# The last 1024 tokens of an attention and two-MLP kernel: gate and value as one 2x2 block product with seven multiplications

## The chip, the core and the metric

One core of a Trainium2 chip runs the whole program. The metric is device time in microseconds (us) of one launch, the median of several runs; lower is better. Beside it stands one profiled execution, from which every row below is taken. TensorE (PE, with its weight loads as PEld) multiplies; VectorE (DVE), ScalarE (ACT) and GpSimd (POOL) do the rest; SyncE (SP) issues all DMAs.

## The reference, cut to what matters

```python
# q, k, v: (4, 8, 576, 64) float32; attention over a window of 64 positions
scores = scale * np.matmul(q, k.transpose(0, 1, 3, 2))
scores = np.where((rel >= 0) & (rel < 64), scores, -1e9)
attn = np.exp(scores - max); attn = attn / (attn.sum(-1) + 1e-9)
x = (attn @ v) as (2304 tokens, 512)
# first MLP, d_ff = 1536; the weights are float64
x = (1 / (1 + np.exp(-(x @ w_gate)))) * (x @ w_val) @ w_out
# second MLP
out = ((x @ w_a) * (x @ w_b)) @ w_out2
```

## The kernel before

**Numbers in two parts.** Each MLP operand is held as a high part (`h`) and the remainder (`l`) in fp32r. A product `w x` is three matmuls: high by high, high by low, low by high (`product`, L299 to L309). The float64 weights come in as pairs of 32-bit words and are turned into float32 on the chip (`decode`, L252 to L286: ACT, DVE and POOL), split, used, and also written to DRAM (`kept`). There are 12 chunks of 128 hidden units (`fc`) in each MLP, so 24 decodings of three matrices (gate or `a`, value or `b`, and `o` for out).

**Two halves.** The 2304 tokens are nine blocks of 256. `HALVES` (L32) gives blocks 0 to 4 to the first half, in groups (0), (1, 2), (3, 4), and blocks 5 to 8, the last 1024 tokens, to the second half, in groups (5, 6) and (7, 8). A half runs the first MLP (phase 0) and then the second (phase 1). The first half decodes the weights as it needs them; the second half reads them back from DRAM (`fetch`, L288). A turn of the plan takes one group and three chunks: for each chunk `hidden` (L311) makes gate and value, of 12 matmuls each, one PSUM bank each, with ACT and DVE forming the hidden vector and its two parts; then `projection` (L462) multiplies the hidden parts of the turn before by `o` and adds them to an accumulator in SBUF (`evacuate`, L353). A matmul has 512 columns for a group of two blocks and 256 for a single block. In phase 0 the projection goes block by block with 256 columns, in phase 1 with 512.

**Attention.** 36 units (`attention`, L102: 128 tokens and four heads each) run as generators beside the MLP work. Blocks 0 to 4 come first; those of blocks 5 and 6 are fed in during phase 1 of the first half and those of blocks 7 and 8 at its end and in phase 0 of the second half. A unit ends by writing the two parts of its result, `xh` on ACT and `xl` on DVE (L186, L187).

**Order.** The code is written in one order; the framework's scheduler then lists the instructions of each engine by its own estimate of time, and each engine runs its list strictly in that order. PSUM has eight banks: two for accumulation (`ps_acc`), three for gate and value (`ps_gv`), three for attention (`ps_at`).

Of the kernel before, what the change touches and what calls it, by code (L numbers as in the profile page):

```python
# [8 lines left out]
F32 = mybir.dt.float32  # L9
# [10 lines left out]
def tile_window_attention_gated_mlps(ctx, tc, q, k, v, w1g, w1v, w1o, w2a, w2b, w2o, out):  # L20
    nc = tc.nc
# [10 lines left out]
    HALVES = (((0,), (1, 2), (3, 4)), ((5, 6), (7, 8)))  # L32
    W = 2 * N
    LAG = 1
# [6 lines left out]
    const = ctx.enter_context(tc.tile_pool(name="const", bufs=1))  # L41
    stage = ctx.enter_context(tc.tile_pool(name="stage", bufs=3))
    dec = ctx.enter_context(tc.tile_pool(name="dec", bufs=1))
    wts = ctx.enter_context(tc.tile_pool(name="wts", bufs=G + 1))
    xs = ctx.enter_context(tc.tile_pool(name="xs", bufs=1))
    accp = ctx.enter_context(tc.tile_pool(name="accp", bufs=5))
    hp = ctx.enter_context(tc.tile_pool(name="hp", bufs=5))
    tmp = ctx.enter_context(tc.tile_pool(name="tmp", bufs=2))
    kts = ctx.enter_context(tc.tile_pool(name="kts", bufs=5))
    vs = ctx.enter_context(tc.tile_pool(name="vs", bufs=5))  # L50
    work = ctx.enter_context(tc.tile_pool(name="work", bufs=3))
    small = ctx.enter_context(tc.tile_pool(name="small", bufs=5))
    dram = ctx.enter_context(tc.tile_pool(name="dram", bufs=1, space=bass.MemoryType.DRAM))
    ps_acc = ctx.enter_context(tc.tile_pool(name="ps_acc", bufs=2, space=PSUM))
    ps_gv = ctx.enter_context(tc.tile_pool(name="ps_gv", bufs=3, space=PSUM))
    ps_at = ctx.enter_context(tc.tile_pool(name="ps_at", bufs=3, space=PSUM))
# [9 lines left out]
    mask_n = const.tile([P, P], F32, name="mask_n")  # L66
    mask_0 = const.tile([P, P], F32, name="mask_0")
# [21 lines left out]
    qts = [const.tile([P, 2, 2, 2, WIN], F32, name=f"qt{i}") for i in range(3)]  # L89
# [12 lines left out]
    def attention(t, hq, xhi, xlo, c0):  # L102
# [71 lines left out]
        pt = work.tile([P, 2, 4, WIN], F32, tag="pt", name=f"pt{t}_{hq}")  # L174
# [5 lines left out]
        for i in range(4):  # L180
# [5 lines left out]
        nc.scalar.activation(out=xhi[:, pairs, c0:c0 + P], in_=xps, func=AF.Copy)  # L186
        nc.vector.tensor_tensor(  # L187
            out=xlo[:, pairs, c0:c0 + P], in0=xps, in1=xhi[:, pairs, c0:c0 + P].bitcast(F32), op=ALU.subtract
        )
# [3 lines left out]

    PLACE = {(0,): 0, (1, 2): 1, (3, 4): 2, (5, 6): 3, (7, 8): 1}
# [12 lines left out]
    group_of = {b: g for half in HALVES for g in half for b in g}  # L207

    def attention_units(blk):
        if (0, (blk,)) not in x:  # L210
            new_x(0, group_of[blk])
        for i in range(TB):
            for hq in range(2):
                yield blk, attention(blk * TB + i, hq, *x[0, (blk,)], i * P)
# [21 lines left out]
    staged, ready, kept = {}, {}, {}  # L236

    def load_weights(F):
        ph, fc = divmod(F % (2 * NF), NF)
# [12 lines left out]
    def decode(F):  # L252
# [3 lines left out]
        for nm in "abo":  # L256
# [5 lines left out]
            ex = dec.tile([P, DM], I32, tag="ex", name="ex")  # L262
# [20 lines left out]
            kept[F, nm] = dram.tile([P, 2, DM], F32, tag=f"k{nm}{F}", name=f"k{nm}{F}")  # L283
# [4 lines left out]
    def fetch(F):  # L288

        got = {}  # L290
        for nm in "abo":
            pair = wts.tile([P, 2, DM], F32R, tag=f"w{nm}", name=f"w{nm}")
            nc.sync.dma_start(out=pair.bitcast(F32), in_=kept[F - 2 * NF, nm])
            got[nm] = (pair[:, 0, :], pair[:, 1, :])
        ready[F] = got
        yield


    def product(ps, w, x):  # L299
# [4 lines left out]
        for c in range(NP):  # L304
            for a, b in ((wh, xh), (wh, xl), (wl, xh)):
                nc.tensor.matmul(  # L306
                    ps, lhsT=a[:, c * P:(c + 1) * P], rhs=b[:, c, :], start=(n == 0), stop=(n == 3 * NP - 1)
                )
                n += 1  # L309

    def hidden(phase, w, x):  # L311
# [13 lines left out]
        factor = 0.5 if phase == 0 else 1.0  # L325
        hh = hp.tile([P, W], F32R, tag="hh", name="hh")[:, 0:n]
        hl = hp.tile([P, W], F32R, tag="hl", name="hl")[:, 0:n]
        nc.scalar.activation(out=hh, in_=hr, func=AF.Copy, scale=factor)  # L328
        nc.vector.scalar_tensor_tensor(  # L329
            out=hl, in0=hr, scalar=factor, in1=hh.bitcast(F32), op0=ALU.mult, op1=ALU.subtract  # L330
        )
        return hh, hl
# [54 lines left out]
    def turns(order, half, ph):  # L387
# [3 lines left out]
        def take(group, n):  # L391
            f0 = at[group[0]]
            n = min(n, NF - f0)
# [5 lines left out]
        if (half, ph) == (0, 0):  # L399
            for _, b, fcs in FIRST:  # L400
                take((b,), len(fcs))
        elif ph == 0:
            for g in order:
                for b in g:
                    take((b,), G)
        for j, g in enumerate(order):
            take(g, 1 + j * (G - 1) // (len(order) - 1))
        while any(f < NF for f in at.values()):
# [5 lines left out]
    for half, groups in enumerate(HALVES):  # L414
        order = groups
        for ph in range(2):
            ts = turns(order, half, ph)
            plan.extend((half, ph, g, fcs) for g, fcs in ts)
            order = [g for g, fcs in ts if fcs[-1] == NF - 1]
    base = lambda half, ph: (2 * half + ph) * NF  # L420
# [111 lines left out]
```

## Time and profile before

| | |
|---|---|
| median of 3 runs | 1029.39 us (1029.35 to 1031.32) |
| the profiled execution | 1031.98 us, its span 1030.2 us |
| PE busy | 1008.6 us, 98% of the span, 6278 matmul records |
| DVE, ACT, POOL busy | 543.7, 382.8, 242.0 us |
| chain that ended last | PE 84%, DVE 9%, ACT 3% |
| DMA | 137.64 MB, mean 134 GB/s |

Matmuls overlap in their pipeline, so a busy PE is not PE at its best: the time that one matmul really takes from the stream is the distance between the starts of two neighbours. A record's own length is longer than that.

### The profile page before, as it was taken

How to read it: one execution, taken by the hardware profiler on the slowest of the kernel's cores; microseconds unless marked ns; L12 is line 12 of the kernel's file. 1: busy time of each engine (PE TensorE's matmuls, PEld its weight loads, DVE VectorE, ACT ScalarE, POOL GpSimd, SP SyncE). 2: the span in 40 equal slices, each digit the busy share in tenths (PEclk: the TensorE clock that was granted, in tenths of full speed). 3: DMA queues.
4: the chain of work that ended last, by engine and by line, in shares of the span. 5: the costliest groups of instructions: out<-in, count | busy, mean ns of one | idle time of the engine just before them, and what ended most of it. 6: DMA issues, size and time to landing. Idle time of an engine off the chain costs nothing.

```text
span 1030.2 us, 16412 instructions
## 1 busy us (share of the span) xinstructions
PE 1008.6 (98%) x6278; PEld 887.0 (86%) x6278; DVE 543.7 (53%) x1126; ACT 382.8 (37%) x931; POOL 242.0 (23%) x209
## 2 busy tenths in 40 slices
PE   7899999999999899999999999999999999999998
PEld 6798998989889788888888889988888888888886
DVE  5899468776858975766754354223222221222223
ACT  7887643333334566343321346321111232111110
POOL 2555045433426733333521000000000020000000
PEclk9899999999999999999999999999999999999999
DMA  8998355543534554454524262152232323232102
GB/s 202 246 267 258 68 176 199 177 152 123 205 108 159 164 164 153 142 156 144 205 82 142 86 185 70 42 185 72 74 124 78 123 83 102 82 102 82 62 21 81
DMA packets 114862, 137.64 MB, mean 134 GB/s; under 512 B 62048, under 2 KB 90976, under 8 KB 114784
## 3 DMA queue, kind: packets, MB, share of 16 engines
q1 hardware_dynamic: 114784, 136.60, 42.3%
q8 instruction: 49, 0.80, 0.3%
q14 instruction: 29, 0.24, 0.1%
HBM read 89.65 MB, written 42.47 MB: 128 GB/s over the span
## 4 chain that ended last, share of the span: by engine, by line
PE 84%; DVE 9%; ACT 3%; issue 2%; POOL 2%; DMA 1%; SPq 0%; POOLq 0%; DVEq 0%; ACTq 0%
PE acc L345 26%; PE gps L306 26%; PE vps L306 25%; PE sps L147 2%; PE xps L183 2%; PE tps L173 1%; DVE ex L263 1%; DVE wi L270 1%; DVE ex L275 1%; DVE hl L329 1%; ACT pr L161 1%; PE kqps L120 1%; DVE wi L267 1%; DVE xacc L364 1%; POOL wi L273 1%
## 5 line engine op out<-in xcount | busy, mean ns | idle before, releaser
L306 PE MATMUL gps<-xh,wa 128*128 128x512 f32 (+1 forms) x1056 | 303.8, 355 | 1.0 <-ACT wa L280 1.0
L306 PE MATMUL vps<-xh,wb 128*128 128x512 f32 (+1 forms) x1056 | 301.1, 352 | 0.5 <-ACT wb L280 0.5
L306 PEld LDWEIGHTS gps<-xh,wa 128*128 128x128 f32 x1056 | 190.9, 190 | 27.6 <-ACT wa L280 1.3
L306 PEld LDWEIGHTS vps<-xh,wb 128*128 128x128 f32 x1056 | 190.2, 190 | 27.1 <-ACT wb L280 0.7
L306 PE MATMUL gps<-xl,wa 128*128 128x512 f32 (+1 forms) x528 | 186.7, 354 | 0.8 <-DVE xl L187 0.7
L306 PE MATMUL vps<-xl,wb 128*128 128x512 f32 (+1 forms) x528 | 185.8, 352 | 0.0
L345 PE MATMUL acc<-hh,wo 128*128 128x256 f32 x864 | 166.0, 284 | 1.0 <-DVE xacc L364 1.0
L328 ACT ACTIVATE hh<-hr 128x512 fp32r<-128x512 f32 (+1 forms) x132 | 73.1, 554 | 213.5 <-DVE hr L324 115.2
L345 PEld LDWEIGHTS acc<-hh,wo 128*128 128x128 f32 x864 | 138.2, 191 | 2.8 <-DVE xacc L364 1.1
L345 PE MATMUL acc<-wo,hh 128*128 128x512 f32 x432 | 133.5, 391 | 2.4 <-DVE xacc L364 1.6
L345 PE MATMUL acc<-hl,wo 128*128 128x256 f32 x432 | 122.5, 284 | 1.2 <-DVE hl L329 1.2
L364 DVE TENSOR_TENSOR xacc<-acc,xacc 128x512 f32<-128x512 f32 x130 | 88.1, 688 | 63.2 <-PE acc L345 62.7
L324 DVE TENSOR_TENSOR hr<-vps,hr 128x512 f32<-128x512 f32 (+1 forms) x60 | 38.1, 636 | 150.0 <-PE vps L306 149.3
L273 POOL TENSOR_TENSOR wi<-wi,low 128x512 int32<-128x512 int32 x72 | 98.4, 1366 | 66.1 <-DVE wi L270 42.9
L306 PEld LDWEIGHTS gps<-xl,wa 128*128 128x128 f32 x528 | 100.4, 190 | 13.3 <-DVE xl L187 1.0
L306 PEld LDWEIGHTS vps<-xl,wb 128*128 128x128 f32 x528 | 100.2, 190 | 13.1
L329 DVE SCALAR_TENSOR_TENSOR hl<-hr,hh 128x512 fp32r<-128x512 f32 (+1 forms) x132 | 84.3, 639 | 50.7 <-ACT hh L328 50.3
L321 DVE SCALAR_TENSOR_TENSOR hr<-hr,vps 128x256 f32<-128x256 f32 (+1 forms) x72 | 39.7, 551 | 128.6 <-PE vps L306 125.3
L345 PEld LDWEIGHTS acc<-wo,hh 128*128 128x128 f32 x432 | 80.1, 188 | 19.3 <-DVE xacc L364 1.6
L345 PEld LDWEIGHTS acc<-hl,wo 128*128 128x128 f32 x432 | 82.7, 191 | 2.4 <-DVE hl L329 1.4
L345 PE MATMUL acc<-wo,hl 128*128 128x512 f32 x216 | 83.7, 390 | 0.0
L370 POOL TENSOR_TENSOR xl<-xacc,xh 128x512 fp32r<-128x512 f32 x18 | 25.3, 1419 | 208.7 <-ACT xh L369 208.7
(68 smaller groups left out, 1100.2 us busy)
## 6 DMA issues: line engine op xcount, KB each, us to landing
st_o<-in_moe_w_out_dram SPq DMA_DIRECT2D x24, 512.0 KB, 3.8
ka<-wa SPq DMA_DIRECT2D x24, 512.0 KB, 2.6
kb<-wb SPq DMA_DIRECT2D x24, 512.0 KB, 3.1
ko<-wo SPq DMA_DIRECT2D x24, 512.0 KB, 2.8
wa<-ka SPq DMA_DIRECT2D x24, 512.0 KB, 3.3
wb<-kb SPq DMA_DIRECT2D x24, 512.0 KB, 3.4
wo<-ko SPq DMA_DIRECT2D x24, 512.0 KB, 4.0
st_a<-in_moe_w_gate_dram SPq DMA_DIRECT2D x12, 512.0 KB, 4.3
```

The costliest lines, as they stand in the source:

```text
L120: nc.tensor.transpose(kqps[:, i, j, :], raw[nm][:, 2 * j:2 * j + 2, :], ident)
L147: nc.tensor.matmul(sps[:, s, j, :], lhsT=qt[:, j, s], rhs=kt[:, j, s * WIN:s * WIN + P], start=True, stop=True)
L183: nc.tensor.matmul(xps[rows, i // 2, s * WIN:(s + 1) * WIN], lhsT=vv[:, i, :], rhs=pt[:, s, i, :], start=True, stop=True)
L273: nc.gpsimd.tensor_tensor(out=wi, in0=wi, in1=low, op=ALU.add)
L306: nc.tensor.matmul(ps, lhsT=a[:, c * P:(c + 1) * P], rhs=b[:, c, :], start=(n == 0), stop=(n == 3 * NP - 1))
L321: nc.vector.scalar_tensor_tensor(out=hr, in0=hr, scalar=1.0, in1=vps, op0=ALU.add, op1=ALU.mult)
L324: nc.vector.tensor_tensor(out=hr, in0=vps, in1=hr, op=ALU.mult)
L328: nc.scalar.activation(out=hh, in_=hr, func=AF.Copy, scale=factor)
L329: nc.vector.scalar_tensor_tensor(out=hl, in0=hr, scalar=factor, in1=hh.bitcast(F32), op0=ALU.mult, op1=ALU.subtract)
L345: nc.tensor.matmul(ps, lhsT=a[:, m * P:(m + 1) * P], rhs=b, start=begin and n == 0 and (phase == 1 or m % 2 == 0), stop=end and n == 2 and ...
L364: nc.vector.tensor_tensor(out=dst, in0=ps, in1=dst, op=ALU.add)
L370: nc.gpsimd.tensor_tensor(out=xl, in0=dst, in1=xh.bitcast(F32), op=ALU.subtract)
```

## The change

The code for blocks 5 to 8 is replaced. The first part (`FRONT`, blocks 0 to 4) keeps its plan, except that group (0) stops three chunks short of the end of phase 1.

- **Attention.** All 36 units run in the first part; those of blocks 5 to 8 are paced evenly over the turns from the seventh to the last but two. For these 16 units only one float32 result is written (`xq`, on ACT), without the split.
- **Decoding.** `decode` also stores the float32 of `a` and `b` (`kf`, 48 more DMAs of 256 KB); the buffer `ex` becomes two deep, `pt` goes from three buffers to two.
- **Second pool layout.** `second_part` closes the pools of attention and decoding and opens others in their place.
- **The block product.** The 1024 tokens are two halves of 512 columns; the 512 contraction rows are two halves of 256. Gate and value of a chunk are then a 2x2 product of blocks, made by seven block products in place of eight (`quad`). A block product is six matmuls of 512 columns (`multiply`). Seven operands are formed from x once in each phase (`operands`, tiles of 1024 elements a partition), and for each chunk four combinations of weights (`fetch`: on POOL the sum and the low part, on ACT the high part, tiles of 256). One PSUM bank, `pa`, gathers products 1, 6, 7 and 4 and is copied out by ACT three times on the way (`r1`, `r2`, `r3`).
- **Projection.** Two chunks are projected together, one bank of 512 columns and six matmuls at a time (`bank_sum`); `fill` places these between the products.
- **The last three chunks of group (0)** in phase 1 run between the two phases of the second part.

```diff
-    HALVES = (((0,), (1, 2), (3, 4)), ((5, 6), (7, 8)))
+    FRONT, BACK = ((0,), (1, 2), (3, 4)), (5, 6, 7, 8)
...
+            if nm != "o":
+                nc.sync.dma_start(out=kept[F, "f"][:, i], in_=wf)
...
+    LEFT = {(0, (0,)): NF, (1, (0,)): NF - G}
...
+    def operands(x, places):
+        b11, b21, b12, b22 = x[0, 0], x[1, 0], x[0, 1], x[1, 1]
+        def split(nm, f):
...
+            nc.scalar.activation(out=o[:, 0], in_=f, func=AF.Copy)
+            (nc.gpsimd if len(got) % 3 == 2 else nc.vector).tensor_tensor(
+                out=o[:, 1], in0=f, in1=o[:, 0].bitcast(F32), op=ALU.subtract
+            )
...
+        split(1, b11)
+        t1 = minus(b12, b11, 1)
+        split(5, t1)
+        t2 = minus(b22, t1, 2)
+        split(6, t2)
+        yield got
+        split(2, b21)
+        t3 = minus(b22, b12, 3)
+        split(7, t3)
+        t4 = minus(b21, t2, 4)
+        split(4, t4)
+        split(3, b22)
...
+        def combined(nm, x, y, op):
+            s = late["sts"].tile([P, CH], F32, tag="s", name=f"s{nm}")
+            nc.gpsimd.tensor_tensor(out=s, in0=x, in1=y, op=op)
+            t = late["wq"].tile([P, 2, CH], F32R, tag="wq", name=f"wq{nm}")
+            nc.scalar.activation(out=t[:, 0], in_=s, func=AF.Copy)
+            nc.gpsimd.tensor_tensor(out=t[:, 1], in0=s, in1=t[:, 0].bitcast(F32), op=ALU.subtract)
...
+        s1 = combined(5, b1, b2, ALU.add)
+        s2 = combined(6, s1, a1, ALU.subtract)
+        combined(7, a1, b1, ALU.subtract)
+        combined(3, a2, s2, ALU.subtract)
...
+        prod(1, pa, True)
+        r1 = kept_sum(pa, 1)
+        prod(5, pb, True)
+        prod(6, pa, False)
+        r2 = kept_sum(pa, 2)
+        prod(2, pc, True)
+        nc.vector.tensor_tensor(out=g[0], in0=pc, in1=r1, op=ALU.add)
+        prod(7, pa, False)
+        r3 = kept_sum(pa, 3)
+        nc.vector.tensor_tensor(out=r3, in0=pb, in1=r3, op=ALU.add)
+        fill()
+        prod(4, pa, False)
+        h0 = finish(0, pa)
+        prod(3, pb, False)
+        nc.vector.tensor_tensor(out=g[1], in0=pb, in1=r2, op=ALU.add)
+        return h0, finish(1, r3)
+
+    def bank_sum(dst, pairs, begin):
+        ps = ps_acc.tile([P, W], F32, tag="acc", name="accq")
+        for n, (a, b) in enumerate(pairs):
+            nc.tensor.matmul(ps, lhsT=a, rhs=b, start=n == 0, stop=n == len(pairs) - 1)
+        if begin:
+            nc.scalar.activation(out=dst, in_=ps, func=AF.Copy)
+        else:
+            nc.vector.tensor_tensor(out=dst, in0=ps, in1=dst, op=ALU.add)
```

`finish` forms the hidden vector: in phase 0 tanh on ACT and a product on DVE, in phase 1 the product alone; then the split into two parts on ACT and DVE.

**Place one: ACT in phase 0 of the second part.** Before, in a steady stretch (`hr` is tanh of the gate bank, `hh` the high part of the hidden vector):

```order
L320 ACTIVATE hr_8199<-gps_8173 128x512
L328 ACTIVATE hh_8202<-hr_8199 128x512
L320 ACTIVATE hr_8232<-gps_8206 128x512
L328 ACTIVATE hh_8235<-hr_8232 128x512
L320 ACTIVATE hr_8311<-gps_8285 128x512
```

Now, in a steady stretch (`r1` to `r3` are the copies of bank `qa`; `g0` and `g1` stand for the tanh of a chunk's two token halves; `wq` are high parts of weight combinations; 8004 belongs to one chunk and 8138 and 8135 to the next):

```order
L573 ACTIVATE r1_8146<-qa_8135 128x512
L321 ACTIVATE hh_8059<-g0_8003 128x512
L539 ACTIVATE wq5_8236<-s5_8234 128x256
L580 ACTIVATE g1_8004<-g1_8004 128x512
L580 ACTIVATE g0_8138<-g0_8138 128x512
L573 ACTIVATE r2_8160<-qa_8135 128x512
L321 ACTIVATE h11_8072<-g1_8004 128x512
```

ACT had two instructions for a gate and value pair; now it has the copies, the weights and the tanh in one list, and the copy `r2` of a chunk stands behind the tanh `g0` of the same chunk.

**Place two: PE at the same point.** Before (`vps` is the value bank, `acc` a projection bank):

```order
L306 MATMUL vps<-xh_7_6608,wb 128x512 x2
L306 MATMUL vps<-xl_7_6609,wb 128x512
L306 MATMUL vps<-xh_7_6608,wb 128x512
L345 MATMUL acc_8318<-hh,wo 128x256
L345 MATMUL acc_8318<-hl,wo 128x256
L345 MATMUL acc_8318<-hh,wo 128x256 x2
```

Now (`op1` to `op7` are the operands from x; `qa`, `qb`, `qc` the three banks of a chunk; `accq` a projection bank):

```order
L555 MATMUL qb_8255<-op5_7068,wq5_8117 128x512
L555 MATMUL qc_8256<-op2_7166,wa_8107 128x512 x6
L555 MATMUL qa_8389<-op1_7063,wa_8226 128x512 x4
L555 MATMUL qa_8135<-op7_7171,wq7_7992 128x512 x6
L615 MATMUL accq_8210<-hh_7805,wo_7605 128x512
```

Products of three chunks now stand interleaved; between product 2 and product 7 stand four matmuls of a later chunk's product 1.

## Rows read from the trace of the kernel before

**Rows 1.** The page's first part: busy us, share, instructions.

```profile
PE 1008.6 (98%) x6278; PEld 887.0 (86%) x6278; DVE 543.7 (53%) x1126; ACT 382.8 (37%) x931; POOL 242.0 (23%) x209
```

**Rows 2.** Stretches: length, busy PE, PEld, DVE, ACT, POOL; clock, DMA share, GB/s.

```profile
0.00:600.00 600.00, 582.57 (x3846) 516.67 (x3847) 418.10 (x880) 285.12 (x718) 230.90 (x198) 0.99 0.53 163
600.00:700.00 100.00, 100.00 (x811) 93.20 (x810) 36.25 (x116) 39.97 (x119) 0.89 (x3) 1.00 0.38 117
700.00:1000.00 300.00, 299.73 (x1512) 255.96 (x1511) 79.72 (x116) 54.64 (x89) 10.24 (x8) 1.00 0.27 86
```

**Rows 3.** Timeline at 900 us: start, length, engine, line, instruction.

```profile
900.53 0.39 PE L306 MATMUL gps<-xh,wa 128*128 128x512 f32 x1
900.53 0.19 PEld L306 LDWEIGHTS vps<-xh,wb 128*128 128x128 f32 x1
900.76 0.39 PE L306 MATMUL vps<-xh,wb 128*128 128x512 f32 x1
...
900.98 0.39 PE L306 MATMUL vps<-xl,wb 128*128 128x512 f32 x1
...
901.01 0.60 ACT L323 ACTIVATE hr<-gps 128x512 f32<-128x512 f32 x1 [5.43 <-PE gps L306]
```

**Rows 4.** Timeline at 642 us, matmuls of 256 columns.

```profile
642.37 0.28 PE L306 MATMUL vps<-xl,wb 128*128 128x256 f32 x1
642.49 0.28 PE L306 MATMUL vps<-xh,wb 128*128 128x256 f32 x1
```

**Rows 5.** PE's groups by line and shape: xcount, busy us, mean ns, idle before.

```profile
L306 PE MATMUL gps<-xh,wa 128*128 128x512 f32 x672 | 222.5, 392 | 0.0
...
L345 PE MATMUL acc<-hh,wo 128*128 128x256 f32 x864 | 166.0, 284 | 1.0 <-DVE xacc L364 1.0
L345 PE MATMUL acc<-wo,hh 128*128 128x512 f32 x432 | 133.5, 391 | 2.4 <-DVE xacc L364 1.6 <-ACT xacc L362 0.7
...
L306 PE MATMUL gps<-xh,wa 128*128 128x256 f32 x384 | 81.3, 291 | 1.0 <-ACT wa L280 1.0
```

**Rows 6.** What PE waited for: us in total, times, longest us.

```profile
PE xps L183 <- ACT pt L175: 3.5, 2, 2.1
PE acc L345 <- DVE xacc L364: 2.6, 4, 1.4
```

**Rows 7.** DVE and ACT groups between 850 and 1000 us.

```profile
L364 DVE TENSOR_TENSOR xacc<-acc,xacc 128x512 f32<-128x512 f32 x20 | 13.5, 692 | 12.7 <-PE acc L345 12.7
...
L328 ACT ACTIVATE hh<-hr 128x512 fp32r<-128x512 f32 x19 | 12.0, 633 | 54.1 <-DVE hr L324 54.1
L323 ACT ACTIVATE hr<-gps 128x512 f32<-128x512 f32 x19 | 11.4, 600 | 68.1 <-PE gps L306 68.1
```

**Rows 8.** ACT at 256 elements, POOL at 512 and 128, whole span.

```profile
L328 ACT ACTIVATE hh<-hr 128x256 fp32r<-128x256 f32 x48 | 20.0, 417 | 46.0 <-DVE hr L321 28.5 <-DVE hr L324 17.3
...
L370 POOL TENSOR_TENSOR xl<-xacc,xh 128x512 fp32r<-128x512 f32 x18 | 25.3, 1419 | 208.7 <-ACT xh L369 208.7
L126 POOL COPY kt<-kt 128x128 f32<-128x128 f32 x32 | 14.0, 437 | 82.4 <-ACT kt L122 74.9 <-DVE den L168 2.9 <-DVE nmax L156 2.6
```

**Rows 9.** Timeline at 860 us: DVE, then ACT that waits for it.

```profile
860.23 0.69 DVE L324 TENSOR_TENSOR hr<-vps,hr 128x512 f32<-128x512 f32 x1 [3.35 <-PE vps L306]
...
860.95 0.63 ACT L328 ACTIVATE hh<-hr 128x512 fp32r<-128x512 f32 x1 [2.86 <-DVE hr L324]
```

**Rows 10.** Stretches: L170's instructions (one a unit); all engines at 300 us.

```profile
0.00:600.00 600.00, 26.84 (x30) 0.99 0.53 163
...
300.00:350.00 50.00, 47.76 (x326) 44.12 (x324) 42.48 (x54) 21.31 (x41) 33.75 (x25) 1.00 0.49 164
```

**Rows 11.** DVE at L170 and L364: ns min/median/max, first and last start.

```profile
L170 DVE TENSOR_TENSOR pr<-pr,den x36: 681/692/1782, 10.4 to 640.3; 128x512 f32<-128x512 f32 x36
...
L364 DVE TENSOR_TENSOR xacc<-acc,xacc x130: 673/692/693, 96.9 to 1026.5; 128x512 f32<-128x512 f32 x130
```

More of the change, by code (lines that the diff above doesn't have):

```diff
@@ L324, in hidden @@
             nc.vector.tensor_tensor(out=hr, in0=vps, in1=hr, op=ALU.mult)
[L325 to L332, printed above, removed]
+        h = tuple(hp.tile([P, W], F32R, tag=f"h{p}", name=f"h{p}")[:, 0:n] for p in "hl")
+        split_hidden(phase, h, hr)
+        return h
     def project(phase, acc, w, h, begin, end):
@@ L385, in tile_window_attention_gated_mlps, with turns @@
     )
-    def turns(order, half, ph):
+    LEFT = {(0, (0,)): NF, (1, (0,)): NF - G}
+    def turns(order, ph):
         at = {b: 0 for g in order for b in g}
@@ L392, in take @@
             f0 = at[group[0]]
[L393 removed]
+            n = min(n, LEFT.get((ph, group), NF) - f0)
             if n:
@@ L397, in take @@
                 at[b] = f0 + n
-        if (half, ph) == (0, 0):
+        if ph == 0:
             for _, b, fcs in FIRST:
                 take((b,), len(fcs))
[L402 to L405, printed above, removed]
         for j, g in enumerate(order):
             take(g, 1 + j * (G - 1) // (len(order) - 1))
-        while any(f < NF for f in at.values()):
+        for _ in range(NF // G):
             for g in order:
@@ L413, in tile_window_attention_gated_mlps @@
     plan = []
[L414 to L420, printed above, removed]
+    order = FRONT
+    for ph in range(2):
+        ts = turns(order, ph)
+        plan.extend((ph, g, fcs) for g, fcs in ts)
+        order = [g for g, fcs in ts if fcs[-1] == NF - 1]
     last_use = {}
-    for n, (half, ph, _, fcs) in enumerate(plan):
+    for n, (ph, _, fcs) in enumerate(plan):
         for fc in fcs:
-            last_use[base(half, ph) + fc] = n
-    NW = 4 * NF
+            last_use[ph * NF + fc] = n
+    NW = 2 * NF
     nload, ndec, dec_it = [0], [0], [None]
@@ new lines, in tile_window_attention_gated_mlps, with job @@
+    PAIR = 2
+    y, hs = {}, []
+    for n, (ph, fc) in enumerate(steps):
+        ahead(n + 1)
+        w = fetched[n]
+        if ph is None:
+            hs.append((w, hidden(1, w, x[1, (0,)])))
+            if fc == NF - 1:
+                projection(1, 0, hs, False, True)
+                hs = []
+            continue
+        if fc == 0:
+            res = [accp.tile([P, 2, W], F32, tag="xacc", name=f"res{ph}{i}") for i in range(4)]
+        hs.append((w["o"], quad(ph, w, x_ops, fill)))
+        if len(hs) < PAIR:
+            fill(-(-len(rest) // 2))
+            continue
+        fill(len(rest))
+        begin, end = fc == PAIR - 1, fc == NF - 1
+        if ph == 0:
+            for i, j in ((0, 0), (0, 1), (1, 1), (1, 0)):
+                y[i, j] = res[2 * i + j]
+                for c in range(2):
+                    sl = slice((2 * i + c) * P, (2 * i + c + 1) * P)
+                    pairs = [
+                        (o[a][:, sl], h[j][b]) for o, h in hs for a, b in ((0, 0), (0, 1), (1, 0))
+                    ]
+                    rest.append(lambda d=res[2 * i + j][:, c], p=pairs, b=begin: bank_sum(d, p, b))
+        else:
+            for i in range(2 * NP):
+                j, sl = i // NP, slice(i % NP * P, (i % NP + 1) * P)
+                pairs = [(h[j][a][:, sl], o[b]) for o, h in hs for a, b in ((0, 0), (0, 1), (1, 0))]
+                def job(d=res[i // 2][:, i % 2], p=pairs, b=begin, e=end, r=BACK[0] * N + i * P):
+                    bank_sum(d, p, b)
+                    if e:
+                        nc.sync.dma_start(out=out[r:r + P, :], in_=d)
+                rest.append(job)
+        hs = []
+        if end:
+            fill(len(rest))
+            if ph == 0:
+                built = operands(y, (PLACE[plan[-2][1]], PLACE[plan[-1][1]]))
+                next(built)
+                x_ops = next(built)
```

220 lines of the change are left out of this document (157 added, 63 removed).

## The prediction

> **What bounds the kernel now.** I read the page's busy times first: PE is busy for 98% of the span, the next engine for 53% [rows 1]; then the stretches [rows 2]. From 700 to 1000 us PE is busy for 299.7 of 300 us at the full granted clock, while DVE is busy for 80; from 0 to 600 us, where decoding and attention run, PE is busy for 582.6 and DVE for 418. What PE waited for is small change: the largest entry is 3.5 us in two waits [rows 6]. So the span is PE's stream of matmuls, and a matmul costs the distance to its neighbour's start. For 512 columns that is 0.45 us over two starts, from 900.53 to 900.98, taken as 0.226 each, and the weights of the next one load during the first 0.19 us of it, at no cost [rows 3]. For 256 columns it is 0.120 us [rows 4]: half the columns cost more than half, so wide matmuls are cheaper per column too.
>
> The MLPs' matmuls, from the groups [rows 5] and by the factor with which the listed group enters (vps equals gps, and each low-part group has half as many): 512 columns, 3 x 672 + 1.5 x 432 = 2664; 256 columns, 3 x 384 + 1.5 x 864 = 2448. At 0.226 and 0.120 that is 602.1 + 293.8 = 895.9 us of the span of 1030.2. The rest is the start, attention's matmuls and waits.
>
> **The change part by part.**
>
> *Fewer and wider matmuls.* In the new order the MLPs have 2952 matmuls of 512 columns and 1584 of 256. Two things do that: 24 chunks lose six of 48 product matmuls each (144 of 512 columns), and all the remaining work on the 1024 tokens that was 256 wide becomes 512 wide. 2952 x 0.226 + 1584 x 0.120 = 667.2 + 190.1 = 857.3 us. **Gain 38.6 us**, on the bounding engine. Attention's matmuls stay as they are.
>
> *What the other engines get.* A chunk of the second part takes PE 66 matmuls (42 products, 24 projections), 66 x 0.226 = 14.9 us. Beside it stand, with durations from quiet stretches [rows 7, 8]: on DVE three sums, two products, two low parts and four accumulations, 11 x 0.69 = 7.6 us; on ACT three copies of 0.60, two tanh of 0.60 in phase 0, two high parts of 0.63 and four of 0.42, 5.9 us; on POOL eight operations of 256 elements, for which no row stands: they lie between a copy of 128 (0.44) and an operation of 512 (1.42), I take 0.7, so 5.6 us (3.5 to 11.4). No engine is full. As work this costs nothing; its cover is the 14.9 us of PE, and what can cost is order.
>
> *The bank that is read three times.* Product 6 may not write `pa` before ACT has copied it, nor 7, nor 4. A copy takes: last matmul to its end 0.39 us, of which 0.226 is its own slot; 0.09 to ACT's start (900.92 to 901.01); 0.60 [rows 3]; and about 0.06 back to PE, as DVE to ACT takes 0.03 [rows 9]. That is 0.91 us, and six matmuls placed between cover 1.36. Where ACT comes free in time, nothing is lost. In phase 0 it doesn't in five of the twelve chunks: ACT's list puts the tanh `g0` ahead of copy `r2` (one such place is shown above), and `g0` waits for DVE's sum of product 2. From the end of product 2: 0.25 to DVE, 0.69, 0.03, tanh 0.60, copy 0.60, 0.06 = 2.23 us, while PE has four matmuls (0.90) until product 7. It then stands for 1.33 us, **five times: 6.6 us**. In phase 1 there is no tanh and the copy waits for nothing late. I walked one pair of chunks (132 matmuls, 29.8 us) through the lists of PE, ACT and DVE with these durations: besides that place, only two accumulations find their bank 0.1 to 0.2 us late, because DVE works off its list in order. Twelve pairs at 0.3: **3.6 us** (0 to 10).
>
> *Starts of the second part and of its phase 1.* Each forms seven operands of 1024 elements: seven ACT copies (from 0.42 at 256 and 0.63 at 512, an estimated 1.06), nine DVE operations (at most twice 0.69) and two on POOL (at most twice 1.42). That is up to 12.4 us of DVE in a chain from the last accumulation to product 3. Its cover at phase 1 is the three chunks of group (0): 72 x 0.120 + 18 x 0.226 = 12.7 us; at the first start, the last two turns. The products need the operands one after another, so most is hidden; ACT's list at the first start has weight parts that wait for DMA and POOL ahead of the last decoding's split. I take **4 us** for both (0 to 14).
>
> *The first part.* 30 of 36 attention units already ran before 600 us [rows 10], so only six move in. They cost DVE less than the 36 us that it was busy in all from 600 to 700 us, when they ran [rows 2]; 16 low-part writes go. DVE rises there from 418 us in 600 to 454 in some 615 at most, 70% to 74%, and the clumps become even. On the other side, at 300 us, with DVE at 42.5 of 50 us, PE fell to 47.8 [rows 10]. The 48 new stores are 12.6 MB beside 163 GB/s x 600 us = 98 MB at a DMA share of 0.53 [rows 2]: hidden, unless SP's list holds one up and DVE waits for `ex`; that buffer is two deep now. I take **2 us** (-4 to 14).
>
> *The end* is the same chain, an accumulation and a store: nothing.
>
> The sum: the profiled execution took 1031.98 us (span 1030.2 and 1.8 around it). 1031.98 - 38.6 + 6.6 + 3.6 + 4 + 2 = 1009.6; it stands 2.6 us over the median, so the median becomes **1007 us**, a gain of 2.2%.
>
> **The rivals.**
>
> *All of it hidden* (chance 0.12). For: PE's waits before were 1 to 3 us in all per cause [rows 6]. Against: the in-order wait at `r2`, worked out above. 1007 - 16.2 = 991 us.
>
> *POOL holds DVE up in the second part* (0.13). POOL was idle from 600 us on before; now it runs for 5.6 of 14.9 us. A DVE operation with both inputs in SBUF took 0.681 us at best and 1.782 at worst, 36 times, while one that reads a PSUM bank never took more than 0.693 in 130 [rows 11]; the long ones lie in the time when POOL works. The page SBUF — State Buffer of the Trainium skill, section Who interferes with whom, says that a DVE instruction with two SBUF inputs contends with a GpSimd instruction that reads SBUF, and one with at most one SBUF input does not; by that rule three or four of DVE's eleven operations of a chunk would be exposed, and the rows agree with both halves of it. Worked out from rows: three such operations, each up to one POOL operation late (0.7), is up to 2.1 us a chunk; if 0.5 us of it reaches PE, 24 x 0.5 = 12 us: 1019 us.
>
> *The first part becomes DVE's* (0.10). If the even pacing makes all of 100 to 600 us like the stretch at 300 us, 2.2 us are lost in each 50: 22 us, less some 9 that such places cost already: 1020 us.
>
> *Slower than before: ACT's list* (0.08). Seventy-two copies of `pa` each stand in a list with up to ten other instructions. One instruction of 0.60 ahead of a copy makes it 1.51 us against a cover of 1.36; two make it 2.11, 0.75 over. If that is the rule, as at the five places, PE stands 72 x 0.75 = 54 us: 1007 - 10 + 54 = 1051 us, the 10 being the waits of this kind in the forecast. It decides from 38.6 / 72 = 0.54 us a copy. Against: ACT has 9 us free in each 14.9 and in the pair that I walked five of six copies came in time.
>
> *A milder form of the same*, about 0.3 us a copy (0.05), with the starts at their upper bound would leave the time where it is: 1007 - 10 (the waits of that kind that the forecast holds) + 22 + 10 = 1029 us.
>
> That the change doesn't do what it says is not among them: the counts come from the new order itself.
>
> **How the numbers follow.** The forecast, 1007 us, has 0.52, for 1000 to 1013. With all hidden below (991) and POOL and the first part above (1019, 1020), 0.87 lies under 1027. The range 993 to 1023 leaves out half of the hidden case, the slower ones and little of the two above: about 0.2. About 0.2% (2 us) is what a measurement of this kernel can tell from no change. Faster by more: 0.52 + 0.12 + 0.13 + 0.10 = 0.87; within: 0.04; slower: 0.09.
>
> **What would show it.** Matmul starts 0.226 us apart in the products, and 144 matmuls of 512 columns fewer in the sum of work: the gain. PE idle before product 7 of L555 with ACT as the releaser, about 1.3 us, only in phase 0: the `r2` place; the same spread over all copies and phases: the slower rival. DVE operations of the split (L322) at 1 to 1.5 us with POOL busy: POOL's rival. PE gaps ended by DVE or ACT's weights before 600 us: the first part. Less than 80% of the second part's DVE operations at 0.69 us would make my walk wrong, and so would products waiting for DMA, which the walk takes to have landed long before: the weights of a chunk come in more than a chunk ahead.

## The result and the profile after

The changed kernel takes 1005.99 us, median of four runs (1004.78 to 1007.33); the kernel before, beside it on the same chip, 1029.68. The ratio is 0.9767, 95% interval 0.975 to 0.9784. The profiled execution has a span of 1004.6 us, 25.6 less than before.

The page's busy times, to be read against [rows 1], and two stretches (length, then busy PE, PEld, DVE, ACT, POOL with instructions, the clock, the DMA share, GB/s), against [rows 2]:

```profile
PE 976.6 (97%) x5702; PEld 834.7 (83%) x5702; DVE 626.0 (62%) x1212; ACT 445.5 (44%) x1069; POOL 400.9 (40%) x397
```

```profile
0.00:600.00 600.00, 577.77 (x3946) 510.43 (x3947) 416.64 (x935) 308.52 (x803) 249.95 (x218) 0.99 0.61 186
600.00:1004.60 404.60, 398.82 (x1758) 324.28 (x1756) 209.32 (x278) 136.96 (x266) 150.95 (x179) 1.00 0.40 138
```

PE still sets the end (78% of the chain that ended last, 84% before). It has 576 fewer records. In the first 600 us it stands 4.8 us longer than before (577.77 against 582.57), with DVE as busy as before. From 600 us on DVE, ACT and POOL have far more to do than they had, and PE hardly waits for them. This is the whole list of what PE waited for from 600 us on (in all, times, longest); in the kernel before it was 0.4 us in two waits:

```profile
PE qa L555 <- POOL op L497: 0.7, 1, 0.7
PE acc L355 <- DVE res L619: 0.6, 2, 0.4
PE accq L615 <- DVE res L619: 0.6, 1, 0.6
PE qa L555 <- ACT r L573: 0.2, 1, 0.2
```

The copies of the bank that is read three times cost 0.2 us in the whole run, in one wait at 840 us, in phase 1. The forecast had put 6.6 us there, all of it in phase 0.

**Where the 25.6 us are.** (The medians are 23.7 us apart; the profiled execution of the kernel before, 1031.98 us, lay above its median.) I took the distance from each matmul's start to the next one's over the whole trace, and set 0.226 and 0.120 us against it as the prediction does. What is over is called a wait where it is more than 0.03 us, and a stretch where it is less. The first part is counted to 680 us of the kernel before, past its last attention unit, and to the first product of the changed one. A matmul that ran at half the granted clock counts as a wait in this way, for instance about 1.5 us at 191 us in the changed kernel, 1.4 us at 53 us in the kernel before.

| us | forecast | measured |
|---|---|---|
| fewer and wider matmuls (counts as forecast) | -38.6 | -38.6 |
| waits in the second part (`r2` 6.6, banks 3.6, starts 4) | +14.2 | +2.2 |
| matmuls further apart than 0.226, no wait | none | +6.6 |
| first part: waits +7.9, attention's matmuls -3.6 | +2 | +4.3 |
| sum | -22.4 | -25.5 |

The sum came out close partly by luck, because errors of opposite sign met: 12 us of waits that don't exist on one side, and 6.6 us of a slower stream that the forecast didn't have and 2.3 us more in the first part on the other. The experiments go after both, and after the first part.

### The profile page after: what moved, and what is told of

Its sections match the earlier page's. It is cut to its first block, busy times and chain, and to the rows that moved or that the text cites. A ratio compares the mean times of both kernels' runs of the same rounds, so it can differ in the third digit from the quotient of the medians.

```text
span 1004.6 us, 15877 instructions
## 1 busy us (share of the span) xinstructions
PE 976.6 (97%) x5702; PEld 834.7 (83%) x5702; DVE 626.0 (62%) x1212; ACT 445.5 (44%) x1069; POOL 400.9 (40%) x397
## 4 chain that ended last, share of the span: by engine, by line
PE 78%; DVE 9%; DMA 5%; ACT 4%; issue 3%; POOL 1%; SPq 0%; DVEq 0%; POOLq 0%
PE acc L355 13%; PE qa L555 13%; PE accq L615 13%; PE gps L312 13%; PE vps L312 12%; PE qb L555 6%; PE qc L555 3%; DMA kf<-ex 2%; DVE ex L278 2%; PE sps L143 1%; ACT pr L157 1%; DVE ex L290 1%; PE xps L179 1%; DMA vb<-v 1%; DVE wi L285 1%
## 5 line engine op out<-in xcount | busy, mean ns | idle before, releaser
L312 PE MATMUL gps<-xh,wa 128*128 128x512 f32 (+1 forms) x624 | 176.0, 350 | 1.9 <-ACT wa L295 1.9
L312 PE MATMUL vps<-xh,wb 128*128 128x512 f32 (+1 forms) x624 | 171.7, 343 | 2.3 <-ACT hr L335 2.3
L540 POOL TENSOR_TENSOR wq<-s,wq 128x256 fp32r<-128x256 f32 x96 | 77.8, 814 | 149.9 <-ACT wq L539 149.8
L312 PEld LDWEIGHTS vps<-xh,wb 128*128 128x128 f32 x624 | 111.7, 191 | 16.0 <-ACT hr L335 2.5
L312 PEld LDWEIGHTS gps<-xh,wa 128*128 128x128 f32 x624 | 111.4, 190 | 15.8 <-ACT wa L295 2.0
L312 PE MATMUL gps<-xl,wa 128*128 128x512 f32 (+1 forms) x312 | 107.2, 344 | 1.6 <-POOL xl L380 1.1
L312 PE MATMUL vps<-xl,wb 128*128 128x512 f32 (+1 forms) x312 | 106.6, 342 | 0.0
L355 PE MATMUL acc<-hh,wo 128*128 128x256 f32 x480 | 92.4, 285 | 2.4 <-DVE xacc L374 2.4
L555 PE MATMUL qa<-op,wq 128*128 128x512 f32 x288 | 77.2, 395 | 0.7 <-POOL op L497 0.7
L555 PE MATMUL qb<-op,wq 128*128 128x512 f32 x288 | 75.0, 394 | 0.0
```

What stands on the lines that cost most here:

```text
L312: nc.tensor.matmul(ps, lhsT=a[:, c * P:(c + 1) * P], rhs=b[:, c, :], start=(n == 0), stop=(n == 3 * NP - 1))
L355: nc.tensor.matmul(ps, lhsT=a[:, m * P:(m + 1) * P], rhs=b, start=begin and n == 0 and (phase == 1 or m % 2 == 0), stop=end and n == 2 and ...
L540: nc.gpsimd.tensor_tensor(out=t[:, 1], in0=s, in1=t[:, 0].bitcast(F32), op=ALU.subtract)
L555: nc.tensor.matmul(ps, lhsT=a[:, c * P:(c + 1) * P], rhs=b[:, c, :], start=first and n == 0, stop=n == 5, skip_group_check=True,)
```

## The experiments

The kernel before ran beside each; medians of it lay at 1029.9 to 1030.7 us.

**One product more, and the copies twice.** The first asks what a product costs in this stream, the second how much cover the copies have.

```diff
         prod(2, pc, True)
+        prod(2, pc, True)
         nc.vector.tensor_tensor(out=g[0], in0=pc, in1=r1, op=ALU.add)
```

> The changed kernel with product 2 of every chunk computed twice into the same bank: 144 matmuls of 512 columns more, the count that eight block products would have, everything else as it is. Theory A (PE's stream is the bound in the second part, a matmul costs its distance to the next one): 144 x 0.2265 to 0.2334 = 32.6 to 33.6 us more, 1039 us. Theory B (part of the stream stands in waits that the extra product would cover): clearly under 30 us more.

```diff
             nc.scalar.activation(out=r, in_=ps, func=AF.Copy)
+            nc.scalar.activation(out=r, in_=ps, func=AF.Copy)
             return r
```

> The changed kernel with each of the 72 copies of bank pa on ACT made twice, so that each takes 0.5 to 0.6 us longer: 36 to 43 us more of ACT. Theory A (the copies have ample cover, since the order puts 6 to 16 matmuls of other products between a copy and the product that waits for it; the forecast's wait at r2 was misread): within 3 us of 1006. Theory B (the copies are close to their cover, as my walk had it: 0.91 of 1.36 us in the best case, so that 0.5 more is 0.05 to 0.15 over, and more where ACT's list is late): 72 x 0.1 to 0.5 = 7 to 36 us more.

With the product 1037.9 us (ratio to before 1.0075, 1.0059 to 1.0091): 31.9 us more for 144 matmuls, 0.222 each. An eighth product would have cost the whole gain and more: at its counts the change is slower than the kernel before. That is 0.7 us under the range of theory A and above the 30 us that theory B stays under, so theory A is the nearer one.

With the copies twice 1014.54 us (0.9849, 0.9833 to 0.9866): 8.5 us more for 36 to 43 us of ACT. That is over A's 3 us and at the low end of B's range. What PE waited for from 600 us on in that run:

```profile
PE qa L555 <- ACT r L574: 4.5, 3, 2.0
PE accq L616 <- DVE hl L322: 1.1, 1, 1.1
```

So the copies are covered as they stand, and most of the added time is too, but their cover is not without end. All three of those waits lie ahead of product 4, which has to wait for `r3`; two of them are 2 us long, and behind the one at 845 us the granted clock fell to half for 3.4 us. The scheduler also listed the second part anew for the longer copies, so the run shows the cover in an order like this one, not in the very same.

**Why matmuls stand further apart.** In the changed kernel the 1008 products stood 0.2334 us apart and the projections 0.2307, with no idle time shown. The granted clock was 1.00, and the mean distance of products (those under 0.26) was 0.231 to 0.233 whether DVE, ACT or POOL was busy at that moment or not. But it was the same in every chunk for a given product: 0.234 for products 3 and 7, 0.229 for 4. Three runs separate what they read: all products with one weight and one operand, with one weight, and with one operand, in this order. The other operands or weights are formed and left unread, so these kernels compute something else:

```diff
-        prod = lambda n, ps, first: multiply(ps, w[n], x[n], first)
+        prod = lambda n, ps, first: multiply(ps, w[4], x[4], first)
```

```diff
-        prod = lambda n, ps, first: multiply(ps, w[n], x[n], first)
+        prod = lambda n, ps, first: multiply(ps, w[4], x[n], first)
```

```diff
-        prod = lambda n, ps, first: multiply(ps, w[n], x[n], first)
+        prod = lambda n, ps, first: multiply(ps, w[n], x[4], first)
```

> The changed kernel with all seven products of a chunk made from the weights and the operand of product 4 (their own are formed as before and not used): the same banks, counts and copies, wrong numbers. In the changed kernel products 3 and 7 have matmuls 0.234 us apart in every chunk, product 4 0.229, product 1 0.233; with the pad the products still stand 0.2323 apart, so the 32 bytes explain 1 of 7 us. Theory A (which buffers in SBUF, or which numbers, a matmul reads sets its distance): all products come to 0.227 to 0.229 and 4 to 6 us go. Theory B (the short groups, banks and waits set it): products 3 and 7 stay at 0.233 to 0.234, time within 2 us of 1006.

> The changed kernel with all seven products of a chunk made from the weights of product 4, each with its own operand (wrong numbers, same banks, counts and copies). With one operand and one weight for all of them the products stood 0.2267 us apart in steady stretches (660 to 780 us) and the projections too, against 0.232 and 0.230 in the changed kernel. Theory A (the weights: those that ACT and POOL have just formed, and the waits for them): 0.2267 to 0.228 here. Theory B (the seven operands): 0.231 to 0.233. The start of a phase is late here, as it was there, since the order now begins with other products; the distances of the steady stretches decide.

> The reverse: each product of a chunk with its own weights and all with the operand of product 4 (wrong numbers). Theory A (the weights set the distance): 0.231 to 0.233 in steady stretches. Theory B (the operands do): 0.2267 to 0.228.

A fourth only exchanges buffers of operands:

```diff
-    OPS = {1: None, 5: None, 6: None, 2: "xh", 7: "xl", 4: "xh", 3: "xl"}
+    OPS = {1: None, 5: None, 6: None, 2: "xl", 7: "xh", 4: "xl", 3: "xh"}
```

> The changed kernel with the operands of products 2 and 7 in each other's buffer, and those of 4 and 3, nothing else. Theory A1 (the buffer of the operand sets the distance between matmuls): products 3 and 7 fall from 0.234 to 0.228 to 0.231, and 2 and 4 rise to 0.233 to 0.234. Theory A2 (their weights, which come from the combinations, or the numbers themselves): the distances stay with the products: 3 and 7 at 0.234, 4 at 0.229. The time stays within 1.5 us of 1006 in either case.

With one weight and one operand, the products stood 0.2267 us apart from 660 to 780 us and the projections too: theory A as to the distances. The kernel as a whole took 1028.31 us, not less, since every product then waits for the operand that is formed next to last. This is what PE waited for most in the profiled execution (1023.29 us, the fastest of ten), and it says what a start of a phase costs when its order is not covered:

```profile
PE qa L555 <- ACT op L496: 11.6, 2, 9.6
```

That is not the whole price: from 800 to 850 us, where the longest of these waits lies, the granted clock was 0.90 in the mean.

With the buffers exchanged nothing moved, in time (1004.91 us) or in distance: 3 and 7 stayed at 0.234 and 4 at 0.229. So it was not these buffers. With one weight products stood 0.232 apart (1018.64 us in one run), with one operand 0.231 (1013.5): by its letter the first speaks for the operands and the second for the weights, so neither side alone is the cause. Split by where the two operands begin in SBUF, both runs agree. Pads in the second part move nothing but that: PE, DVE and ACT ran the same instructions in the same order as in the changed kernel. The first pad, of 32 bytes (`[P, 8]`), was run before these three, the second, of 96 (`[P, 24]`), after them, together with the earlier store that stands under the first part below:

```diff
         early.close()
+        pad = ctx.enter_context(tc.tile_pool(name="pad", bufs=1, side="right", reuse_waits="tile"))
+        nc.gpsimd.memset(pad.tile([P, 8], F32, name="pad"), 0.0)
```

> The changed kernel with a pad of 32 bytes opened ahead of the pools of the second part, and nothing else. In the profile of the changed kernel the 1008 products stand 0.2334 us apart, not 0.2265, and the 576 projection matmuls 0.2307. In the built program the tiles of ops and wq begin 32 bytes off a multiple of 64, all other operands of wide matmuls on one; split by that, matmuls whose moving operand and weights differ in it stand 0.2338 apart (430 of them), those with both at 32 0.231, those with both at 0 0.228 to 0.230. Theory A (the place of the operands in SBUF): with all of them at a multiple of 64 the products come to 0.228 to 0.2295, 4 to 5.5 us off, and some of the 2 us lost on the others with it: 1000 to 1003 us. Theory B (short groups of six matmuls, each in a bank of its own and with waits, disturb the stream): pitches stay at 0.233, time within 1 us of 1006.

> The changed kernel with a pad of 96 bytes ahead of the pools of the second part, so that every operand and weight of a wide MLP matmul begins on a multiple of 128 bytes, and with the store of the float32 weights ahead of the other (as in e4). The pad of 32 bytes had left ops and wq 64 bytes off a multiple of 128: there matmuls whose two sides differ in it stood 0.2327 to 0.2331 apart and those with both at 0 0.2283. Theory A (the offset within 128 bytes sets the distance): all products at 0.2267 to 0.228 and the projections, which were only disturbed by their neighbours, at 0.2267 to 0.228: 1008 x 5.5 to 6.5 ns and 576 x 2.5 to 4 ns = 7 to 9 us, and 1.4 us from the store as before: 996 to 998 us. Theory B (the offset explains only what the pad of 32 bytes gave, the rest is short groups and their waits): products at 0.232, 1002 to 1004 us.

And the other way round, in the kernel before:

```diff
+    pad = ctx.enter_context(tc.tile_pool(name="pad", bufs=1))
+    nc.gpsimd.memset(pad.tile([P, 8], F32, name="pad"), 0.0)
     xs = ctx.enter_context(tc.tile_pool(name="xs", bufs=1))
```

> The kernel before with a pad of 32 bytes between the pool of the weights and that of x, and nothing else: in the built program one side of every wide MLP matmul, operand or weights, then begins 32 bytes off a multiple of 64 and the other on one. Theory A (such a difference costs 3.8 to 5.5 ns a matmul, as the groups of the changed kernel had it): 2664 matmuls x 3.8 to 5.5 ns = 10 to 15 us more than 1030. Theory B (the pad in the changed kernel took 1.1 us from 1008 products, so about 1 ns, and the rest of the distance has another cause): 1 to 3 us more.

The table joins the starts in each trace with the addresses in the built program: the offset of a matmul's moving operand and of its weights within 128 bytes, the number of matmuls of 512 columns, and their mean distance in ns (waits over 260 ns left out).

```
kernel          line     moving  weights  count   ns
before          L306        0       0     1960   227.4
before shifted  L308       32       0     1960   233.3
before shifted  L347        0      32      618   233.3
changed         products    0       0      287   229.7
changed         products    0      96      288   233.6
changed         products   96       0      142   233.5
changed         products   96      96      284   231.3
changed         projection  0       0      569   229.3
pad of 32       products    0       0      287   228.3
pad of 32       products    0      64      288   233.1
pad of 32       products   64       0      142   232.7
pad of 32       products   64      64      284   230.0
one weight      products    0       0      563   230.1
one weight      products   96       0      420   234.2
one operand     products    0       0      421   227.4
one operand     products    0      96      571   233.6
pad of 96       products    0       0     1001   226.8
pad of 96       projection  0       0      569   226.9
```

Wherever the two differ in the offset, the distance is 0.2327 to 0.2342, whichever of the two is off and by 32, 64 or 96 bytes. Where all of a kernel's second part is at 0, it is 0.2267 to 0.2269. Those at 0 in a mixed kernel lie between, 0.2274 to 0.2301, and so do the projections, whose own operands were at 0 all the time: only their neighbours differ. Those with both at 64 or both at 96 stood 0.2300 and 0.2313 apart, but only in mixed kernels; a kernel with all of them at one offset other than 0 was not run. With the pad of 96 bytes operand and weights also differ by 256 bytes in 431 products, and these stood no further apart (0.2268); a difference of 128 bytes occurred in none of the kernels, so whether the unit is 128 or 256 bytes is not shown.

That is also why the exchange moved nothing: its buffers all begin at 0, while the weights `wq` begin 96 bytes off, and `ops` too. And it is why product 4 was the best one: its weights are `wb`, at 0. The page TensorE: Matmul & The Clock Gate of the Trainium skill, section Step-by-step: what each phase is for, gives the engine two read ports into SBUF, one for the moving operand and one for weights, so that loading the next weights takes nothing from the running matmul. By that rule I would not expect the place of the weights beside that of the operand to matter. The rows agree with it where both begin at a multiple of 128 bytes; elsewhere it does matter, and the measurement decides. Whether it is the weight load that slows the matmul, no run here shows.

One hundred us of each kernel, with nothing but products and projections in it, first the changed one, then the one with the pad of 96 bytes (length, busy PE with instructions, clock, DMA share, GB/s):

```profile
870.00:970.00 100.00, 100.00 (x435) 1.00 0.34 116
```

```profile
870.00:970.00 100.00, 100.00 (x443) 1.00 0.29 100
```

PE reads as full in both, and does eight matmuls more in the second. The same for the kernel before, 850 to 1000 us, as it was and shifted:

```profile
850.00:1000.00 150.00, 150.00 (x663) 1.00 0.24 78
```

```profile
850.00:1000.00 150.00, 150.00 (x645) 1.00 0.22 75
```

In times: the pad of 32 bytes took 1003.7 us (0.9739, 0.9725 to 0.9754), with its products at 0.2323, so near theory B in the distance, while the time lies between the two; the pad of 96 took **998.96 us** (0.9699, 0.9681 to 0.9717), faster than both kernels and 5.6 us less than with the earlier store alone (1004.59, below), with 6.4 us in the distances of products and projections: theory A, and a time 1 us over its range, since the 1.4 us of the store that both its theories took over did not show. The kernel before with the shift took 1038.42 us (1.0074, 1.0057 to 1.0091), 8.5 more. That is between its theories: by the distances the 512-wide matmuls cost 15.5 us more, as theory A has it, but the 256-wide ones together 6.9 us less: with the same difference of 32 bytes these stood 0.117 apart, without it 0.120. So what holds for 512 columns does not hold for 256; why is open. PE's order came out different in places up to 115 us in this run; behind that it is the same. In the first pad's expectation theory A named multiples of 64; the rows with 64 beside 0 show that this is not enough.

**The first part.** DVE waits there for the buffer `ex`, which POOL and now also a store must have read. The store first, or none:

```diff
+            if nm != "o":
+                nc.sync.dma_start(out=kept[F, "f"][:, i], in_=wf)
             nc.scalar.activation(out=wh, in_=wf, func=AF.Copy)
             nc.gpsimd.tensor_tensor(out=wl, in0=wf, in1=wh.bitcast(F32), op=ALU.subtract)
             got[nm] = (wh, wl)
             nc.sync.dma_start(out=kept[F, nm], in_=pair.bitcast(F32))
-            if nm != "o":
-                nc.sync.dma_start(out=kept[F, "f"][:, i], in_=wf)
```

> The changed kernel with the store of the float32 weights (kf) issued ahead of the store of the two parts and not behind it, in the first part. In the profile of the changed kernel DVE stood 20.3 us in 13 waits for kf to be read out of the buffer ex, and PE lost 11 us more over its nominal distances in the first 600 us than the kernel before did, most of it at 160 to 200 and 360 to 380 us. Theory A (that store holds ex, ex holds DVE's list, and PE's waits at 165 to 190 us come of it): DVE's waits for kf go under 8 us, and 3 to 6 us come back: 1000 to 1003. Theory B (DVE's list is full there anyway, with decoding, attention and the hidden work): DVE waits elsewhere, time within 1 us of 1006.

```diff
-            if nm != "o":
-                nc.sync.dma_start(out=kept[F, "f"][:, i], in_=wf)
...
-            nc.sync.dma_start(out=pair.bitcast(F32), in_=kept[F, nm])
+            nc.sync.dma_start(out=pair.bitcast(F32), in_=kept[F, "a" if nm == "f" else nm])
```

> The changed kernel without the 48 stores of the float32 weights; the second part reads the stored parts in their place, so its products are of wrong numbers while every instruction of the second part stands as it was. 12.6 MB of DMA less and no store that holds the buffer ex. Theory A (the stores hold DVE up in the first part): 3 to 6 us less than 1006, most of it before 200 us, DVE's 20.3 us of waits for kf gone. Theory B (DVE waits for POOL's low part of the weights at the same buffer anyway, 28.4 us in 14 waits): under 1.5 us.

```diff
-    SPAN = range(len(FIRST) + 1, len(plan) - 2)
+    SPAN = range(len(FIRST) + 3, len(plan) - 2)
```

> The changed kernel with the even pacing of the last 16 attention units begun two turns later, so that the first of them no longer fall at 158 to 200 us. In the profile of the changed kernel DVE is busy for 33.9 of 40 us from 160 to 200 us and PE for 34.8, and three units lie there where the kernel before had none; PE lost 7.9 us there over its nominal distances, 1.6 in the kernel before. Theory A (attention on top of decoding and hidden work fills DVE's list there): 4 to 6 us come back at 160 to 200, of which up to 2 are lost again further on, where the units stand closer: 1001 to 1004 us. Theory B (the stores of the float32 weights are the cause, attention is not): within 1 us of 1006.

The store first took 1004.59 us (0.9753, 0.9738 to 0.9769), no store 1004.82 (0.9754, 0.9741 to 0.9767), attention later 1006.48 (0.9769, 0.9755 to 0.9782). None is told apart from 1005.99. With the store first PE, DVE and ACT kept the order of the changed kernel; without stores the scheduler's order came out different up to 165 us. What DVE waited for at `ex`: the changed kernel, the store first, no store.

```profile
DVE ex L278 <- POOL wa L296: 28.4, 14, 4.0
DVE ex L278 <- DMA kf<-ex: 20.3, 13, 3.8
```

```profile
DVE ex L278 <- POOL wa L298: 31.5, 15, 4.3
DVE ex L278 <- DMA kf<-ex: 16.4, 10, 3.1
```

```profile
DVE ex L278 <- POOL wa L296: 32.6, 16, 4.1
```

Without any store DVE waits for POOL a little longer and the 20 us change the time by about 1: theory B. With the store first 16.4 us of the waits stayed, where theory A wanted under 8, and the time is 0.4 us under theory B's range, 1.6 over A's. Putting off attention moved the losses and didn't remove them, as its theory B has it, though the stores that this theory blamed are not the cause either. From 160 to 200 and 360 to 380 us (columns as in [rows 2]), before, changed, and attention later:

```profile
160.00:200.00 40.00, 38.84 (x262) 35.90 (x261) 31.21 (x49) 14.10 (x26) 18.64 (x15) 1.00 0.54 185
360.00:380.00 20.00, 19.86 (x117) 16.39 (x116) 16.89 (x44) 13.48 (x36) 9.54 (x10) 1.00 0.65 194
```

```profile
160.00:200.00 40.00, 34.81 (x215) 31.30 (x214) 33.92 (x65) 19.28 (x47) 19.48 (x16) 0.96 0.64 207
360.00:380.00 20.00, 16.56 (x114) 14.68 (x113) 19.15 (x22) 9.54 (x19) 15.23 (x12) 1.00 0.59 199
```

```profile
160.00:200.00 40.00, 35.09 (x217) 30.92 (x216) 32.98 (x48) 14.66 (x27) 20.87 (x15) 0.98 0.69 227
360.00:380.00 20.00, 17.51 (x124) 15.97 (x123) 18.06 (x32) 10.40 (x26) 13.34 (x10) 0.91 0.53 172
```

PE loses where DVE is at 33 to 34 of 40 us, or 18 to 19 of 20, in all four rows of the two kernels with the change, with the attention units there or without. What fills DVE at 160 to 200 us, and why the kernel before passes there with 31, these runs don't settle; of the 7.9 us of added waits in the first part, neither the stores nor the two turns of attention is the cause by itself.

## Why the prediction was right, point by point

**The gain on PE: right.** The counts were those of the new order, 2952 and 1584, and the run with one product more put the price of a matmul at 0.222. **Work of the other engines at nothing: right.** From 600 us on they are busy for 52%, 34% and 37%, and PE's waits from there on are 2.1 us by the list above. POOL's 256-element operations, taken as 0.7, run 0.81 in the page's `wq` group. Of the second part's 258 DVE operations of 512 elements 225 (87%) took 0.67 to 0.69 us, so the sign by which the walk would be wrong, under 80%, did not show.

**The `r2` place: wrong, 6.6 us for nothing.** The step that failed is "while PE has four matmuls (0.90) until product 7": I took the product 2 that stands ahead of product 7 in PE's list for that of the same chunk. Its bank is `qc_8256`; the product 7 behind it goes to `qa_8135`, whose own product 2 is in `qc_8137`. With numbers, the order reads (lines between left out):

```
L555 MATMUL qc_8137<-op2_7166,wa_7972 128x512 x6
...
L555 MATMUL qa_8135<-op6_7073,wq6_7987 128x512
...
L555 MATMUL qc_8256<-op2_7166,wa_8107 128x512 x6
L555 MATMUL qa_8389<-op1_7063,wa_8226 128x512 x4
L555 MATMUL qa_8135<-op7_7171,wq7_7992 128x512 x6
```

The chunk's product 2 stands ahead of its product 6, so `g0` is early although it stands ahead of the copy, and 22 matmuls lie between product 6 and product 7. One of these places in the trace, PE, DVE and ACT (start, length, engine, line, instruction, in brackets the idle time before it and what ended it):

```profile
690.88 0.68 DVE L600 TENSOR_TENSOR g<-qc,r 128x512 f32<-128x512 f32 x1
691.06 1.23 ACT L580 ACTIVATE g<-g 128x512 f32<-128x512 f32 x2 [0.30 <-DVE g L608]
...
692.14 0.40 PE L555 MATMUL qa<-op,wq 128*128 128x512 f32 x1
692.38 1.32 PE L555 MATMUL qb<-op,wq 128*128 128x512 f32 x5
...
692.58 0.60 ACT L573 ACTIVATE r<-qa 128x512 f32<-128x512 f32 x1 [0.29 <-PE qa L555]
```

Both tanh end at 692.29, and the copy waits 0.29 us more, for PE's product 6. The order was as forecast; the wait behind it was not there.

**The banks, 3.6 us, and the starts, 4: too much.** There was one wait of 0.6 us for `accq`, and 0.7 and 0.6 us around the start of phase 1; at the first start PE shows no wait. Together with `r2` these made 14.2 of forecast waits against 2.2 measured over those of before. I had taken single late places for a rule of every pair.

**A matmul at 0.226 everywhere: wrong, 6.6 us.** The price was read at 900 us of the kernel before, where every operand begins at a multiple of 128 bytes; the new pools `ops` and `wq` begin 96 bytes off one. The step that failed is taking that distance over to operands in other places without a reason; 1008 products at 0.2334 and 576 projections at 0.2307 are what stood there. The pad gives it back, 6.4 us by the distances.

**The first part, 2 us: 4.3,** within its bounds of -4 to 14. The rival by which all of it would go like 300 us didn't come; single stretches did, as above. From 160 to 200 us the granted clock had a mean of 0.96: behind a wait of PE of 2.3 us (for ACT's `hr`, at 188 us) it fell to half for 3.4 us, and matmuls of 256 columns stood 0.213 apart there for 0.120.

**POOL's rival: its mechanism came, its price didn't.** The page SBUF — State Buffer of the Trainium skill, section Who interferes with whom, has DVE instructions with two SBUF inputs contend with POOL; these are the second part's, from 640 to 1000 us (min, median, max in ns):

```profile
L322 DVE SCALAR_TENSOR_TENSOR hl<-g,hh x23: 681/1230/1236, 646.0 to 989.8; 128x512 fp32r<-128x512 f32 x23
L585 DVE TENSOR_TENSOR g<-r,g x12: 680/1225/1228, 832.5 to 990.4; 128x512 f32<-128x512 f32 x12
L322 DVE SCALAR_TENSOR_TENSOR h<-g,h x23: 676/692/810, 649.8 to 992.9; 128x512 fp32r<-128x512 f32 x23
L619 DVE TENSOR_TENSOR res<-accq,res x79: 674/692/692, 681.0 to 999.6; 128x512 f32<-128x512 f32 x79
```

The first three have both inputs in SBUF, the last has one in PSUM. Of the 72 with both in SBUF (with `g<-g,r` of phase 0) 31 took 1.2 us, each of them while POOL was at work; of those with one in PSUM none did. The rows agree with the page so far. But POOL was also at work beside 14 that were not slowed that much, 13 of them `h<-g,h`, of which the longest took 0.81; why these were spared, no run shows. PE's list of waits holds none of it: DVE had the time.

**ACT's rival** (1051) needed 0.75 us at each of 72 copies; it was 0.2 us in all, and even a second copy at each took 8.5 us in all.

## What to carry to other kernels

Before a copy that stands behind something is priced as a wait, follow the numbers of the buffers: the neighbour in the list may belong to another turn of the loop, and the scheduler may already have put other work between. A busy share of 100% says nothing of how far apart matmuls start; compare the number of them in 100 us between two kernels. Where new pools are opened, look at where they begin: 96 bytes of padding were worth 6.4 us here by the distances, about a quarter of what the whole change had brought.

## What the runs showed of the chip that I had not expected

- Matmuls of 512 columns in fp32r stood 0.2267 to 0.2269 us apart where the moving operand and the weights begin at a multiple of 128 bytes and those of all their neighbours do too, and 0.233 to 0.234 where the two differ by 32, 64 or 96 bytes. Neighbours of such matmuls were slower as well (0.2274 to 0.2301). Matmuls of 256 columns with a difference of 32 bytes were not slower: 0.117 against 0.120.
- ACT's instructions of about 0.60 us that had nothing to wait for overlapped, the next starting 0.49 to 0.53 us behind: the copy at 692.58 and the next two at 693.07 and 693.60, as these rows of the changed kernel show. In the walk of the prediction I had put them end to end.

```profile
693.07 0.62 ACT L321 ACTIVATE h<-g 128x512 fp32r<-128x512 f32 x1
693.60 0.40 ACT L539 ACTIVATE wq<-s 128x256 fp32r<-128x256 f32 x1
```
